# Threshold attention into Fourier mixing: the first stretch's bank-emptying additions move between the exponentials and the maskings

## The chip, the cores and the metric

The kernel runs on one core of a Trainium2 chip. The metric is device time in microseconds of one execution. The kernel before takes 1631.21 us, the median of 3 runs (1630.87 to 1632.28). The profiled execution took 1630.36 us, and its span from the first to the last instruction is 1628.5 us.

Engines are called by the profile's names: PE is TensorE (PEld its weight loads), DVE is VectorE, ACT is ScalarE, POOL is GpSimd, SP issues the transfers.

## What is computed

Two blocks follow one another, for 8 batches of 576 rows:

```python
scores = scale * q @ k.T                    # 8 heads of 64, 576 x 576
thresh = max(scores) - tau
scores = where(scores >= thresh, scores, -1e9)
attn = exp(scores - max(scores));  attn = attn / (sum(attn) + 1e-9)
x = attn @ v                                # heads put side by side: 576 x 512
mixed = real(fft(fft(x, axis=1), axis=2))   # "mixing"
u = x + mixed
un = (u - mean(u)) / sqrt(var(u) + 1e-6)
out = u + relu(un @ w_ch1) @ w_ch2          # 512 -> 2048 -> 512, "channels"
```

All of it is in fp32.

## The kernel before, in words

**Attention.** Two heads make a pair and four pairs a batch. A pair is worked off in five steps (`t` is 0 to 4), each for 128 query rows of both heads (the fifth holds the last 64 rows of both). Steps are numbered `i`, 20 to a batch, 160 in all. In a step of the main loop (from batch 2 on, `i` from 40) this is done:

- `scores(i)` (L427, L433): PE writes the scores of the two heads into two PSUM tiles `sc`. The tag has two buffers, so the next step's scores need the tiles of this step back.
- `softmax_first(i)`: DVE takes the row maxima `neg` (L506), ACT the exponentials `e` (L512) and, between the two of them, the threshold `thr` (L516).
- `softmax_second(i)`: DVE masks the exponentials by comparing `sc` with `thr`, and sums them into `den` (L527, "the maskings"); then it adds 1e-9 (L531) and takes the reciprocal (L534).
- `softmax_third(i)`: ACT multiplies the weights by the reciprocal (L540).
- `weights_in_parts(i - 1)`: PE transposes the weights of the step before (`pe` L578, `pw` L596), and ACT copies them out (L584, L598).
- `values_in_parts`, at `t` 1 and 3: PE multiplies by v (`pv`, L627), ACT copies the result to `x` (L634). For the first pair of a batch the target is called `x_first`.

**Channels.** The two products of the channel block are done in groups of 512 rows. All but the first group are done by a two-level fast scheme with seven products on each level (`two_level`). The first half of a group makes units `ph` (L1163, 8 matmuls, one bank): each bank is emptied by an ACT copy, or by a DVE addition into `hs` (`add`, L1100) that an ACT relu follows (L1105). The second half makes units `po` (L1304, 8 matmuls, seven units to a product): a bank is emptied after units 3 and 6, by an ACT copy (L1319) or a DVE addition (L1321, L1324). Beside them run jobs with no bank: sums of h for the next product (L1144, L1121, L1109, on DVE and POOL; kept in `side` for a unit's slot), the closing additions of a group (L1211 on POOL, L863 on DVE; kept in `pending`, two for each `tick()`, or in `side`), and after unit 3 of the first four products `rows.load`, which transposes 128 rows of u (`pn`, L836), copies them (L841, L842) and takes their statistics (L844, L845).

**Mixing.** When a batch's attention is done, `mixing(b)` makes its Fourier transform in units: three that fold the rows on DVE (L709, L710, L731 to L740), then matmuls `py` (L750) and `pa` (L767, L771), then sums into `u_t` (L787 to L796). The first is put out at the step with `i % 20 == 2`, by `start_batch`.

**The order of the work.** The schedule is written by hand: each engine runs its instructions in the order in which the Python code puts them out. What fills the PE between the attention's own matmuls is put out by `fill()`, three times in a step ("stretches"). Each call raises a `budget` by `per_slot`, takes one unit of the mixing if there is one (`mix(1)`), and then takes channel units from `work` until `spent`, counted in PE columns, has reached the budget. A `ph` unit counts 4096 columns, a `po` unit 2048, a py or pa unit `MIX / 11`. The main loop puts out, in a step:

```python
scores(i); next(values, None)               # PE: sc, and pv at t 1 and 3
softmax_first(i); softmax_second(i)
next(values, None)                          # ACT: x <- pv
fill()                                      # first stretch
next(weights, None)                         # pe and pw of the step before
fill()                                      # second stretch
next(weights, None); softmax_third(i)       # second pw, then the scaling
fill()                                      # third stretch
```

The small banks (tag `mm`: pe, pw, pv, ph, po, py, pa, pn) go round four buffers in the order in which they are asked for. The second `pw` is asked for before the second stretch, though its matmuls come after it.

Of the kernel before, what the change touches and what calls it, by code (L numbers as in the profile page):

```python
# [47 lines left out]
def kernel(  # L48
# [368 lines left out]
    def scores(i):  # L417
        n, t = divmod(i, NT)
        qT, kT = heads[n][0:2]

        nh = 2 if t < 4 else 1
        sc = [ps.tile([128, 2, 512], FP32, tag="sc", name=f"sc{j}") for j in range(nh)]
        if t < 4:
            for c in range(2):
                for j in range(2):
                    hp, k0 = slice(64 * j, 64 * j + 64), D * (1 - j)
                    nc.tensor.matmul(  # L427
                        sc[j][:, c, 0:HALF], qT[hp, 128 * t : 128 * t + 128],
                        kT[hp, k0 + HALF * c : k0 + HALF * (c + 1)], start=True, stop=True,
                    )  # L430
        else:
            for c in range(2):
                nc.tensor.matmul(  # L433
                    sc[0][:, c, 0:HALF], q_ends[:, :], kT[:, D + HALF * c : D + HALF * (c + 1)],
                    start=True, stop=True,
                )
        steps[i] = (sc, nh)
# [84 lines left out]
    def softmax_second(i):  # L522
        sc, nh, e, thr = steps[i]
        den = sb.tile([128, 2], FP32, tag="den", bufs=3, name="den")
        for j in range(nh):
            ej = e[:, S * j : S * (j + 1)].rearrange("p (c n) -> p c n", c=2)
            nc.vector.scalar_tensor_tensor(  # L527
                out=ej, in0=sc[j][:, :, 0:HALF], scalar=thr[:, j : j + 1], in1=ej,
                op0=ALU.is_ge, op1=ALU.mult, accum_out=den[:, j : j + 1],
            )  # L530
        nc.vector.tensor_scalar(  # L531
            out=den[:, 0:nh], in0=den[:, 0:nh], scalar1=1e-9, scalar2=None, op0=ALU.add
        )
        nc.vector.reciprocal(den[:, 0:nh], den[:, 0:nh])  # L534
        steps[i] = (nh, e, den)

    def softmax_third(i):
        nh, e, den = steps[i]
        for j in range(nh):
            nc.scalar.activation(  # L540
                out=e[:, S * j : S * (j + 1)], in_=e[:, S * j : S * (j + 1)], func=ACT.Copy,
                scale=den[:, j : j + 1],
            )
        if nh == 1:
            nc.scalar.copy(e[:, S : S + 64], e[:, 512:S])
        steps[i] = (e, None)
# [495 lines left out]
    def block(g, second, index):  # L1042

        n = len(LOADS) * (g - 1) + (7 if second else 0) + index // PER
        if index % PER == 0:
            ensure(n + 2 if g > 1 or second or index < 20 else n + 1)
        return w1[n % 3][:, 512 * (index % PER) : 512 * (index % PER + 1)]
# [14 lines left out]
    def two_level(g, rows):  # L1062
# [44 lines left out]
        def s1_part(part):  # L1107
            c = slice(512 * part, 512 * part + 512)
            nc.gpsimd.tensor_tensor(  # L1109
                out=s1_tile[:, c], in0=quadrant(0, 1)[:, c], in1=quadrant(1, 1)[:, c], op=ALU.add  # L1110
            )
# [88 lines left out]
                s1_part(part)  # L1200
        for _ in forms:
            pass
        while pending:
            tick()
        if g == 1:
            for part in range(4):
                s1_part(part)
# [41 lines left out]
        side = {}  # L1249
# [45 lines left out]
        for at, m in enumerate(L1):  # L1295
            for jn, j in enumerate(J):
                cut = g == NG - 1 and m == 3
                if jn in (0, 4) or cut and jn > 4:
                    bank = ps.tile([128, 512], FP32, tag="mm", bufs=4, name="po")
                c0 = 0 if cut and jn > 4 else 128 * (jn % 4)  # L1300
                to = bank[:, c0 : c0 + 128]
                right_ = block(g, True, 7 * at + jn)
                for s in range(4):
                    nc.tensor.matmul(  # L1304
                        to, lefts[m][j][:, s], right_[:, 128 * s : 128 * (s + 1)],
                        start=(jn in (0, 4) or cut and jn > 4) and s == 0, stop=s == 3,
                        skip_group_check=True,
                    )
                if jn in (3, 6) or cut and jn > 3:
                    first, end = (0, 512) if jn == 3 else (512, NV)  # L1310
                    if cut and jn > 3:
                        first, end = 128 * jn, 128 * jn + 128
                    src = bank[:, 0 : end - first]

                    def here(v):
                        return v[:, first:end]

                    if m in (1, 5, 4):
                        nc.scalar.copy(here({1: v_u, 5: v_22, 4: v_21}[m]), src)  # L1319
                    elif m == 2:  # L1320
                        V.tensor_tensor(out=here(v_11), in0=here(v_u), in1=src, op=ALU.add)  # L1321
                    else:
                        to = here(v_12 if m == 3 else v_u)
                        V.tensor_tensor(out=to, in0=to, in1=src, op=ALU.add)  # L1324
                for job in side.get((at, jn), ()):
                    job()
                if jn == 3 and at < 4:
                    rows.load((2, 3, 0, 1)[at])
                    if at == 3:
                        wanted.append(rows)  # L1330
                    yield ND * 128
                if jn < 6:
                    yield 2048
            background()
            if m != 3:
                yield 2048
# [14 lines left out]
    pending = []  # L1351
    wanted = []

    def tick():

        for _ in range(2):
            if pending:
                pending.pop(0)()

    def settle(b):  # L1360

# [8 lines left out]
    def background():  # L1370

        if late:
            fold_more()

    late = []
    ended = []


    mixes = []
# [2 lines left out]
    spent = budget = per_slot = 0.0  # L1382
    per_batch = NPAIR * NT

    def fill():
        nonlocal budget, spent
        budget += per_slot
        if mixes and not ended:
            mix(1)
        while work and spent < budget and work[0][0] < mixed:  # L1390
            done = next(work[0][1], None)
            if done is None:
                work.pop(0)
            else:
                spent += done
        if mixes and ended:
            mix(1)

    total = B * per_batch
# [117 lines left out]
    def fold_more():  # L1517
        if folds and next(folds[0], True):
            folds.pop(0)
# [16 lines left out]
    def mix(count):  # L1536
        nonlocal spent, mixed
        for _ in range(count):
            done = next(mixes[0], None)
            if done is None:  # L1540
                mixes.pop(0)
                mixed += 1
                break
            spent += done
# [76 lines left out]
    for i in range(2 * per_batch, total + 3):  # L1621


        n, t = divmod(i, NT)
        values = iter(())
        if i < total:
            scores(i)
        if t == 3 and i < total:
            values = values_in_parts(n, 0)
        elif t == 1 and n > 0:  # L1630
            while folds:
                fold_more()
            values = values_in_parts(n - 1, 1)
        next(values, None)
        if i < total:
            softmax_first(i)
            softmax_second(i)
        next(values, None)
        if i % per_batch == 2:
            for _ in last_fold:  # L1640
                pass
            start_batch(i // per_batch - 1)
        fill()
        if t == 1:
            if n % NPAIR:
                folds.append(fold_rows(n - 1))
            else:
                last_fold = fold_rows(n - 1)
                next(last_fold)
        weights = weights_in_parts(i - 1) if i <= total else iter(())  # L1650
        next(weights, None)
        if t > 2:
            fold_more()
        fill()
        if i % per_batch == 1:
            next(last_fold)
        next(weights, None)
        if i < total:
            softmax_third(i)
            if t == 1:  # L1660
                prep_ends(n)
            if t == 2 and n + 1 < B * NPAIR:
                scale_q(n + 1)
            if t == 3 and n + 1 < B * NPAIR:
                prep_pair(n + 1)
        if wanted:
            wanted.pop().factors()
        if i % per_batch == 1:
            next(last_fold)
        fill()  # L1670
        if t == 2 and n + 1 < B * NPAIR:
            load_v(n + 1)
        if t == 4 and n + 2 < B * NPAIR:
            load_pair(n + 2)
# [50 lines left out]
```

## Time and profile before

| | busy us | share of 1628.5 us |
|---|---|---|
| DVE | 1101.7 | 68% |
| ACT | 907.7 | 56% |
| POOL | 813.2 | 50% |
| DMA queue q1, share of 16 engines | | 48.5% |

PE stands in the prediction's first lines. By time the execution falls into three parts: up to 290 us the first two batches' attention, from 290 to 1385 us the main loop that the change touches, and after it the last groups of the channel block with no attention beside them.

| stretch, us | length | PE busy | DVE busy | mean granted PE clock |
|---|---|---|---|---|
| 0 to 290 | 290.0 | 260.39 | 237.51 | 0.97 |
| 290 to 1385 | 1095.0 | 1063.18 | 719.94 | 0.98 |
| 1385 to 1628.5 | 243.5 | 226.32 | 144.22 | 0.98 |

A row of the profile's groups reads: line, engine, operation, output<-input, shape, count, then busy time, the mean of one in ns, and the idle time of that engine just before such an instruction with the releaser that ended most of it. A row of the timeline reads: start, duration, engine, line, operation, and in brackets the idle time before it with what ended it.

### The profile page before, as it was taken

The numbers are of one execution on the slowest core, as the hardware profiler recorded it, in microseconds if no ns is written. First come the engines' busy times: TensorE is split into PE (matmuls) and PEld (weight loads), VectorE is DVE, ScalarE is ACT, GpSimd is POOL, SyncE is SP. The second block draws the span as 40 slices with busy tenths as digits, with TensorE's granted clock in tenths as the row PEclk, the third lists the DMA queues.
The fourth block names the chain that finished last, engine by engine and source line by source line (L and its number), as shares of the span: only waits on it lengthen the run. The fifth ranks groups of instructions, "written<-read, shape, count | busy, mean of one in ns | idle before, by whom it ended". The sixth has DMA issues, their size and how long they took to land.

```text
span 1628.5 us, 27053 instructions
## 1 busy us (share of the span) xinstructions
PE 1549.9 (95%) x9770; PEld 1194.2 (73%) x9770; DVE 1101.7 (68%) x2165; ACT 907.7 (56%) x1873; POOL 813.2 (50%) x1014
## 2 busy tenths in 40 slices
PE   8998989999999999989999999999998999999997
PEld 4555445556787777877787878877787778879997
DVE  7997786846769466765577566856576666646547
ACT  5774665554555666646665566556665665223131
POOL 6784664034355642545253724554264625546646
PEclk9999999999999999999999999999999999999999
DMA  6423221655846354634554354635464434536655
GB/s 160 125 56 113 74 75 36 196 158 161 266 156 189 102 157 125 187 91 139 139 166 143 112 131 147 178 100 152 126 186 120 136 119 146 209 135 234 239 201 188
DMA packets 245498, 239.04 MB, mean 147 GB/s; under 512 B 196947, under 2 KB 214869, under 8 KB 225014
## 3 DMA queue, kind: packets, MB, share of 16 engines
q1 hardware_dynamic: 242854, 237.02, 48.5%
q8 instruction: 78, 1.28, 0.3%
q10 hardware_dynamic: 2512, 0.30, 0.2%
q14 instruction: 54, 0.44, 0.1%
HBM read 207.50 MB, written 29.62 MB: 146 GB/s over the span
## 4 chain that ended last, share of the span: by engine, by line
PE 67%; DVE 18%; ACT 9%; issue 3%; POOL 2%; DMA 1%; SPq 0%; DVEq 0%; ACTq 0%; POOLq 0%
PE ph L1163 19%; PE po L1304 16%; PE pv L627 8%; PE sc L427 7%; PE pw L596 5%; PE po L901 3%; ACT e L512 2%; PE ph L877 2%; DVE e L527 2%; DVE e L467 2%; DVE hs L1100 2%; PE py L750 1%; DVE neg L506 1%; PE pa L767 1%; ACT hs L1105 1%
## 5 line engine op out<-in xcount | busy, mean ns | idle before, releaser
L506 DVE TENSOR_REDUCE neg<-sc 128x1 f32<-128x576 f32 x216 | 154.2, 751 | 133.9 <-PE sc L427 112.1
L512 ACT ACTIVATE e<-sc,neg 128x576 f32<-128x576 f32 x216 | 158.6, 734 | 152.5 <-DVE neg L506 152.0
L1304 PE MATMUL po<-w,w_all 128*128 128x128 f32 x1792 | 227.9, 277 | 1.0 <-DVE w_all L1144 0.7
L1304 PEld LDWEIGHTS po<-w,w_all 128*128 128x128 f32 x1792 | 213.0, 192 | 10.5 <-issue 8.5
L527 DVE SCALAR_TENSOR_TENSOR e<-sc,thr,e 128x576 f32<-128x576 f32 x216 | 169.1, 816 | 69.6 <-ACT thr L516 69.6
L1109 POOL TENSOR_TENSOR w<-hs 128x512 f32<-128x512 f32 x32 | 41.6, 1303 | 338.4 <-ACT hs L1105 319.2
L1100 DVE TENSOR_TENSOR hs<-ph,hs 128x512 f32<-128x512 f32 (+1 forms) x128 | 105.0, 821 | 140.0 <-PE ph L1163 90.8
L596 PE MATMUL pw<-ident,e 128*128 128x128 f32 x1152 | 175.5, 280 | 21.8 <-ACT x_first L634 11.3
L1163 PE MATMUL ph<-u_t,w 128*128 128x256 f32 x768 | 182.8, 385 | 3.5 <-ACT ends L584 2.0
L598 ACT COPY e_t<-pw 128x512 f32<-128x512 f32 x256 | 148.5, 593 | 65.6 <-PE pw L596 64.6
L427 PE MATMUL sc<-kT,qT 64*128 64x288 f32 x1024 | 169.8, 434 | 9.6 <-DVE e L467 8.3
L596 PEld LDWEIGHTS pw<-ident,e 128*128 128x128 f32 x1152 | 137.7, 144 | 44.0 <-ACT x_first L634 12.9
L1163 PEld LDWEIGHTS ph<-u_t,w 128*128 128x128 f32 x768 | 142.1, 191 | 29.4 <-issue 4.9
L1163 PE MATMUL ph<-w_all,w 128*128 128x256 f32 x672 | 157.0, 382 | 2.9 <-DVE hs L1100 1.8
L540 ACT ACTIVATE e<-e,den 128x576 f32<-128x576 f32 x216 | 157.8, 776 | 2.1 <-DVE den L534 1.7
L1105 ACT ACTIVATE hs<-hs 128x512 f32<-128x512 f32 (+1 forms) x96 | 74.1, 772 | 139.7 <-DVE hs L1100 139.1
L1163 PEld LDWEIGHTS ph<-w_all,w 128*128 128x128 f32 x672 | 123.5, 190 | 25.6 <-issue 5.3
L427 PEld LDWEIGHTS sc<-kT,qT 64*128 64x128 f32 x1024 | 93.3, 187 | 64.0 <-issue 32.1
L1211 POOL TENSOR_TENSOR w_all<-w_all 128x128 f32<-128x128 f32 (+2 forms) x160 | 119.4, 763 | 24.5 <-DVE w_all L1321 11.0
L1304 PE MATMUL po<-w,hs 128*128 128x128 f32 x960 | 130.5, 284 | 0.0
L1304 PEld LDWEIGHTS po<-w,hs 128*128 128x128 f32 x960 | 120.6, 199 | 5.1 <-issue 4.1
L792 POOL TENSOR_TENSOR u_t<-x,tmp 128x289 f32<-128x289 f32 (+1 forms) x45 | 34.9, 775 | 94.3 <-DVE tmp L787 94.3
(221 smaller groups left out, 2980.7 us busy)
## 6 DMA issues: line engine op xcount, KB each, us to landing
w<-f SPq DMA_DIRECT2D x152, 1024.0 KB, 4.9
hs<-in_moe_w_ch_dram SPq DMA_DIRECT2D x23, 512.0 KB, 4.7
q_in<-in_q_dram SPq DMA_DIRECT2D x128, 72.0 KB, 4.0
out_dram<-u SPq DMA_DIRECT2D x36, 256.0 KB, 2.6
k_in<-in_k_dram SPq DMA_DIRECT2D x124, 72.0 KB, 3.0
v_in<-in_v_dram SPq DMA_DIRECT2D x64, 128.0 KB, 4.6
f<-w SPq DMA_DIRECT2D x14, 512.0 KB, 3.4
f<-w SPq DMA_DIRECT2D x7, 1024.0 KB, 4.8
```

Source lines behind the costliest of these rows:

```text
L427: nc.tensor.matmul(sc[j][:, c, 0:HALF], qT[hp, 128 * t : 128 * t + 128], kT[hp, k0 + HALF * c : k0 + HALF * (c + 1)], start=True, stop=True,)
L506: nc.vector.tensor_reduce(out=neg[:, j : j + 1], in_=sc[j][:, :, 0:HALF], axis=AXIS_XY, op=ALU.max, negate=True,)
L512: nc.scalar.activation(out=ej, in_=sc[j][:, :, 0:HALF], func=ACT.Exp, bias=neg[:, j : j + 1], scale=1.0)
L527: nc.vector.scalar_tensor_tensor(out=ej, in0=sc[j][:, :, 0:HALF], scalar=thr[:, j : j + 1], in1=ej, op0=ALU.is_ge, op1=ALU.mult, accum_out ...
L540: nc.scalar.activation(out=e[:, S * j : S * (j + 1)], in_=e[:, S * j : S * (j + 1)], func=ACT.Copy, scale=den[:, j : j + 1],)
L596: nc.tensor.transpose(pw[:, c, :], e[:, c0 : c0 + 128], ident[:, :])
L598: nc.scalar.copy(e_t[:, 4 * j : 4 * j + 4, qs], pw[:, :, :])
L627: nc.tensor.matmul(pv[64 * j : 64 * j + 64, 0:m], vt[:, 2 * c + j, :], e_t[:, 4 * j + c, 0:m] if c < 4 else ends[:, 0, 0:m], start=(c == 0 ...
L1100: nc.vector.tensor_tensor(out=to, in0=bank, in1=to if other is None else other, op=ALU.add)
L1163: nc.tensor.matmul(bank[:, 256 * q : 256 * q + 256].rearrange("p (two n) -> p two n", two=2), left[:, 256 * c + 128 * q : 256 * c + 128 * ...
L1211: return lambda: eng.tensor_tensor(out=to, in0=to, in1=other, op=ALU.add)
L1304: nc.tensor.matmul(to, lefts[m][j][:, s], right_[:, 128 * s : 128 * (s + 1)], start=(jn in (0, 4) or cut and jn > 4) and s == 0, stop=s == ...
```

## The change

In the main loop the first stretch is put out between the exponentials and the maskings. `fill(True)` sets a flag `holding`. While it is set, jobs of `side` and of `pending` are not run when their turn comes but gathered in a list `held`; what is held is put out behind the next unit, and what is left behind the maskings. The mixing's unit is not taken inside such a fill but behind the maskings and the held jobs. So on DVE the additions that empty a bank (and the statistics of `rows.load`, and work that a unit puts out itself) stand between `neg` and the maskings, and the sums of h, the closing additions and the mixing's work behind them. It is for emptying the banks sooner and for giving DVE work while it waits for the exponentials. Outside a held fill the new lists empty at once and the order is as before; the second and third stretch, the first two batches and the end are put out as before. No operation is added or removed.

```diff
-        while pending:
+        while pending or held:
             tick()
+            while held:
+                held.pop(0)()
...
-                for job in side.get((at, jn), ()):
-                    job()
+                while held:
+                    held.pop(0)()
+                held.extend(side.get((at, jn), ()))
+                while held and not holding:
+                    held.pop(0)()
...
     def tick():
 
+        while held:
+            held.pop(0)()
         for _ in range(2):
             if pending:
-                pending.pop(0)()
+                held.append(pending.pop(0))
+        while held and not holding:
+            held.pop(0)()
...
-    def fill():
+    holding = []
+    held = []
+
+    def fill(hold=False):
         nonlocal budget, spent
+        holding[:] = [True] if hold else []
         budget += per_slot
-        if mixes and not ended:
+        if mixes and not ended and not hold:
             mix(1)
         while work and spent < budget and work[0][0] < mixed:
...
+        holding.clear()
         if mixes and ended:
             mix(1)
...
         if i < total:
             softmax_first(i)
-            softmax_second(i)
         next(values, None)
         if i % per_batch == 2:
             for _ in last_fold:
                 pass
             start_batch(i // per_batch - 1)
-        fill()
+        fill(True)
+        if i < total:
+            softmax_second(i)
+        while held:
+            held.pop(0)()
+        if mixes:
+            mix(1)
```

## The prediction

> **What bounds the kernel now.** I read the page first, then what PE waits for in the main loop, then the windows and the chain of waits around its longest waits. The page gives PE:
>
> ```profile
> PE 1549.9 (95%) x9770; PEld 1194.2 (73%) x9770; DVE 1101.7 (68%) x2165; ACT 907.7 (56%) x1873; POOL 813.2 (50%) x1014
> ```
>
> PE is the bound, so only what PE stands still, or runs slowly, can be won. In the main loop (290 to 1385 us) it is idle 1095.0 - 1063.2 = 31.8 us. The waits of PE in that stretch (who waited for whom; total, times, longest):
>
> ```profile
> PE pw L596 <- ACT x_first L634: 11.3, 6, 2.3
> PE py L750 <- DVE f L731: 8.5, 10, 2.0
> PE ph L1163 <- DVE hs L1100: 3.4, 4, 2.0
> PE pw L596 <- DVE hs L1100: 2.4, 2, 2.1
> PE ph L1163 <- ACT ends L584: 2.0, 11, 0.4
> ```
>
> There are two kinds. Rows one and two (19.8 us) lie where a batch's mixing begins (five places, 525 to 1237 us). Rows three to five (7.8 us) are waits for a bank of the first half of a group, scattered. Each longer wait costs again through the clock; windows of 3.41 us (PE busy is the second number, the granted clock the third from the end):
>
> ```profile
> 1052.34:1055.75 3.41, 2.49 (x20) 1.46 (x16) 3.41 (x4) 0.00 (x0) 2.30 (x2) 1.00 0.08 18
> 1055.75:1059.16 3.41, 1.68 (x11) 1.33 (x11) 3.30 (x7) 0.68 (x2) 1.30 (x1) 1.00 0.21 31
> 1059.16:1062.58 3.42, 2.23 (x11) 2.23 (x12) 3.04 (x8) 2.59 (x9) 0.77 (x1) 0.50 0.68 275
> 1062.58:1065.99 3.41, 3.41 (x18) 2.72 (x17) 1.85 (x4) 1.48 (x3) 0.00 (x0) 0.50 0.24 59
> ```
>
> A window in which PE is busy about half leads to a window at half clock; 6.8 us at half clock cost 3.4 us. Four of the five batches (700, 881, 1059, 1236 us) have two such windows, the one at 526 us has one.
>
> The chain of waits there, start and duration:
>
> ```profile
> 1047.30 1.58 DVE e L527 x4
> ...
> 1057.71 0.68 DVE neg L506
> ...
> 1059.30 0.73 ACT e L512
> 1060.03 0.27 ACT x_first L634
> ...
> 1060.35 1.11 PE pw L596 x4
> ```
>
> It is a chain on DVE: without a gap from the maskings at 1047.30 through the mixing's first folds and sums to the next step's `neg`, then exponentials, then `x_first`, which frees the bank that `pw` needs. The scores had been ready since 1051.7 us.
>
> A wait of the second kind, on DVE and then on PE in the timeline:
>
> ```profile
> 427.47 0.75 DVE L506 TENSOR_REDUCE neg<-sc 128x1 f32<-128x576 f32 x1
> 429.21 0.82 DVE L527 SCALAR_TENSOR_TENSOR e<-sc,thr,e 128x576 f32<-128x576 f32 x1 [0.99 <-ACT thr L516]
> 430.34 0.67 DVE L1100 TENSOR_TENSOR hs<-ph,hs 128x512 f32<-128x512 f32 x1
> 431.07 0.68 PE L596 MATMUL pw<-ident,e 128*128 128x128 f32 x2 [2.11 <-DVE hs L1100]
> ```
>
> PE had finished that bank at about 426.7 us; the addition stood behind a masking that waited 0.99 us for its threshold.
>
> [...] L735 takes 1.55 us and L731 1.53 us at 1052 to 1055 us, while POOL runs L1144 and L1121; their shortest are 0.47 and 0.52 us.
>
> **The change, part by part.** It moves work, so PE's busy time at full clock stays.
>
> *Additions ahead of the maskings.* DVE waits for `thr` 69.6 us in 120 steps; that time can hold the addition, but DVE is not the bound, so only PE's waits count. At 407.80 (1.01), 431.07 (2.11), 757.63 (0.27) and 765.81 us (1.95), 5.3 us together, the addition was ready before the maskings and stood behind them. Two maskings with their sums take 1.6 us, `den` 0.4 us, the wait for `thr` 0.4 to 1 us: 2.4 to 3 us, more than each wait. I take 4.8 of the 5.3 us. The eleven waits on ACT `ends` (2.0 us, plus 0.3 at a po unit): the copy stands on ACT behind a relu that waits for such an addition; I take 1.8. The window at half clock from 431.12 us goes with the wait of 2.11 us: 1.7. Sum: 8.3 us.
>
> *Order of mixing and channel unit on PE.* At the step where PE first multiplies for the mixing (`py`, 1053.96 us), the order is now pv, py (waits 0.64 and 1.01 us for DVE), one po unit of 1.06 us, pe, then 2.19 us of idle time until `pw`. The budget of a stretch is (19,240 + 217,088) / 60 = 3939 columns. py counts 1749, so one po unit follows (1749 + 2048 = 3797; three stretches of two units before it overran by 3 x 157, so 3468 suffice). With the mixing behind, two units (4096) go first, and the next stretch gets none. PE thus does one unit of 1.06 us more before the wait ends. If `neg` comes when it comes now, that is 1.06 us for each of five batches.
>
> *When this `neg` comes.* Plus 0.7 us: two steps earlier, the first stretch holds a `rows.load`. Its statistics wait for ACT's copies (until 1038.9 us), and the maskings, now 1035.60 to 1037.16, then come behind them, at about 1039.9 to 1041.5; `den` is ready at 1041.9, so ACT's scaling starts at 1041.9 instead of 1041.31, and behind it the table loads and `rstd` on which DVE waits anyway. Minus 0.4 us: in the step of 1045.50 us a sum of h (L1144, 0.68 us) falls into the wait of 0.39 us for `thr`. Minus 0.5 us: that sum is ready sooner, so POOL's L1144 and L1121 start while DVE masks, which reads PSUM (0.82 us with POOL busy and without)[...]. Bounds: +0.7 and -1.8; I take -0.2. So 5 x 1.26 = 6.3 us.
>
> *Clock at these places.* The idle time falls from 3.84 to about 2.6 us, mostly in one piece. Whether it leads to no, one or two slow windows depends on where their edges fall. I take one fewer in 60% of four batches: 4 x 1.7 x 0.6 = 4.1 us (bounds 0 and 15).
>
> *Maskings later.* They now wait for a PE unit. Behind the masking wait `den`, ACT's scaling, and the next scores for the `sc` tiles. Worst common step: scores at 1101.3, pv, unit from 1104.80 to 1106.7. The maskings, now at 1104.50, would start at 1106.7 + 0.1 + 0.67 = 1107.5 and end at 1109.1; the next scores are at 1111.08 us. Hidden, with 2 us to spare. Without pv the delay is 0.7 to 1.3 us with 2.3 us to spare (1123.92 to 1126.19). With a wide addition (1.22 us), a `rows.load`, or weight forms (L945, L977, which a unit puts out unheld) the margin shrinks to almost nothing. I charge 3 us.
>
> *At no cost:* held closing additions (L863, L1211) and sums of h: needed eight units later or by a store. After 1385 us the order is the old one.
>
> Sum: 8.3 + 6.3 + 4.1 - 3 = 15.7 us; 1631.2 - 15.7 = 1615.5 us.
>
> **Rivals.**
>
> 1. *The mixing's start doesn't move.* DVE's chain gets longer through the statistics, eats the one unit, and the clock drops twice as before. For it: DVE is without a gap there. Against it: the wait for `thr` is in the same chain. Left: 8.3 - 2 = 6 us, so 1625 us.
> 2. *The clock no longer drops.* [...] the idle time falls under half a window: 8.3 + 5 x 2 + 15 - 1 = 32 us, so 1599 us. Against it: `neg` to `pw` alone takes 2.6 us, in which PE has little but pe.
> 3. *The maskings become the bound (slower).* If half of the 120 steps let the scores wait 0.4 us, 24 us are lost against 8.3 us won: 1647 us. For it: margins near 2 us and PE at 97% in the loop. Against it: PE shows no wait for L527 now, and the worst step above still closes.
> 4. *Gain and new waits cancel:* 1631 us.
>
> **How the numbers follow.** Forecast 0.56, rival one 0.22, two 0.08, three 0.08, four 0.06. Faster by over 0.2% (under 1627.9 us): 0.86; within 0.2%: 0.06; slower: 0.08. The range goes from 1602 us (forecast with all of the clock) to 1630 us (only part of the bank waits): it leaves out rivals two and three and part of four.
>
> **What would show it.** Right: the waits of PE for L1100 in the loop fall from 5.8 us to under 1 us and no slow window is left at 431 us; two po units between pv and py at each mixing's start, and fewer slow windows there. Wrong: PE waits for `sc` on L527 (rival three); that step's `neg` still 12.1 us behind the `neg` before it (1045.58 to 1057.71) and two slow windows in each batch (rival one); new waits behind `rows.load` or weight forms beyond 3 us.

## The result and the profile after

The changed kernel takes 1605.7 us (median of 3 runs, 1603.82 to 1607.52) against 1631.21 us (1630.87 to 1632.28): a ratio of 0.9842, 95% interval 0.982 to 0.9864. That is 25.5 us less, where 15.7 us were forecast: the direction was right, the time lies inside the range and near its fast end. A later study with the same kernel gave 1605.14 us and 0.984 (0.9826 to 0.9855).

The profile page's line of busy times, after:

```profile
PE 1537.4 (96%) x9770; PEld 1189.2 (74%) x9770; DVE 1105.6 (69%) x2165; ACT 908.4 (57%) x1873; POOL 811.7 (51%) x1014
```

PE has the same 9770 instructions and 12.5 us less of busy time. No work went, so these 12.5 us were time in which PE's records were longer: at half clock, or behind a wait (shown below). From the first masking of the loop to its last, the kernel before took 1083.6 us (PE idle 31.8), the changed one 1058.6 us (idle 19.8). So 25.0 us were won in the loop; outside it the two traces differ by 0.3 us the other way.

Who PE waited for after, from 290 to 1385 us (total, times, longest):

```profile
PE pw L596 <- ACT x_first L634: 9.1, 5, 2.2
PE pe L578 <- DVE w_all L1326: 5.2, 5, 2.6
...
PE pw L596 <- ACT ends L584: 1.5, 3, 0.5
...
PE ph L1163 <- DVE hs L1100: 0.3, 1, 0.3
```

Line numbers from 1200 to 1326 have moved by two: L1326 is the addition that was L1324. The waits for L1100 fell from 5.8 us to 0.3 us. The waits at the mixing's start are still the longest: the row of `x_first` is only smaller (11.3 before), and a wait of `pe` stands where `py` waited for L731. (A last wait of `py` for L731, 2.9 us at 1384 us, lies behind the loop. The kernel before has it too, 2.6 us at 1410 us, and so outside the stretch of its list.)

The wait that the prediction showed at 431 us, on DVE and PE in the timeline after:

```profile
425.80 0.75 DVE L506 TENSOR_REDUCE neg<-sc 128x1 f32<-128x576 f32 x1
426.47 0.68 DVE L1100 TENSOR_TENSOR hs<-ph,hs 128x512 f32<-128x512 f32 x1
427.50 0.60 PE L596 MATMUL pw<-ident,e 128*128 128x128 f32 x4
428.27 0.81 DVE L527 SCALAR_TENSOR_TENSOR e<-sc,thr,e 128x576 f32<-128x576 f32 x1
```

The addition L1100 now runs directly behind `neg`, while DVE would have waited for the exponentials, and `pw` starts without a wait.

The chain of waits at the mixing's start at 1040 us, after:

```profile
1030.30 1.49 DVE e L527 x4
1031.78 0.02 issue
1031.81 1.18 DVE den L531
...
1038.77 0.68 DVE neg L506
...
1041.09 0.27 ACT x_first L634
1041.36 0.04 issue
1041.40 0.67 PE pw L596 x4
```

It is the same chain as before: DVE without a gap from the maskings to `neg`, then the exponentials, then `x_first`. What changed is how much PE has to do ahead of it: two `po` units (from 1035.64) and `py`, and then it stops twice, close together, for 0.56 us before `pe` and 2.19 us before `pw`: 2.75 us, where it had stopped three times for 3.84 us. This `neg` starts 11.52 us behind the one before it (1027.17 to 1038.69), where it had been 12.13 us (1045.50 to 1057.63).

The windows of 3.41 us there (PE busy is the second number, the granted clock the third from the end):

```profile
1035.08:1038.50 3.42, 3.28 (x28) 2.67 (x24) 3.39 (x9) 0.24 (x1) 0.00 (x0) 1.00 0.25 38
1038.50:1041.91 3.41, 0.81 (x5) 0.56 (x5) 3.41 (x5) 2.38 (x7) 2.07 (x1) 1.00 0.85 346
1041.91:1045.33 3.42, 3.42 (x17) 2.69 (x16) 3.31 (x10) 2.57 (x6) 0.00 (x0) 0.50 0.02 5
1045.33:1048.74 3.41, 3.41 (x27) 3.20 (x27) 1.66 (x3) 1.74 (x4) 1.27 (x1) 1.00 0.44 71
```

One window in which PE was busy for 0.81 us was followed by one window at half clock, where two followed before. In the loop there are four such windows (at 520, 694, 1042 and 1216 us) instead of ten.

### The profile page after: what moved, and what is told of

It reads as the page before. It is cut to its first block, busy times and chain, and to the rows that moved or that the text cites. A ratio compares the mean times of both kernels' runs of the same rounds, so it can differ in the third digit from the quotient of the medians.

```text
span 1603.8 us, 27061 instructions
## 1 busy us (share of the span) xinstructions
PE 1537.4 (96%) x9770; PEld 1189.2 (74%) x9770; DVE 1105.6 (69%) x2165; ACT 908.4 (57%) x1873; POOL 811.7 (51%) x1014
## 4 chain that ended last, share of the span: by engine, by line
PE 76%; DVE 14%; ACT 4%; issue 2%; POOL 2%; DMA 1%; SPq 0%; DVEq 0%; ACTq 0%; POOLq 0%
PE ph L1163 24%; PE po L1306 17%; PE pv L627 8%; PE sc L427 7%; PE pw L596 6%; PE po L901 4%; PE ph L877 2%; PE py L750 2%; DVE e L467 2%; PE sc L433 1%; PE pa L767 1%; PE pe L578 1%; PE pa L771 1%; DVE neg L451 1%; ACT e L512 1%
## 5 line engine op out<-in xcount | busy, mean ns | idle before, releaser
L1100 DVE TENSOR_TENSOR hs<-ph,hs 128x512 f32<-128x512 f32 (+1 forms) x128 | 105.1, 821 | 158.5 <-PE ph L1163 104.0
L596 PE MATMUL pw<-ident,e 128*128 128x128 f32 x1152 | 172.1, 276 | 18.0 <-ACT x_first L634 9.1
L527 DVE SCALAR_TENSOR_TENSOR e<-sc,thr,e 128x576 f32<-128x576 f32 x216 | 168.1, 811 | 17.7 <-ACT thr L516 17.7
L540 ACT ACTIVATE e<-e,den 128x576 f32<-128x576 f32 x216 | 157.6, 775 | 16.6 <-DVE den L534 15.4
L1306 PE MATMUL po<-w,hs 128*128 128x128 f32 x960 | 126.3, 279 | 0.0
L1306 PEld LDWEIGHTS po<-w,hs 128*128 128x128 f32 x960 | 116.2, 193 | 9.4 <-issue 7.2
```

The source lines that it names most:

```text
L527: nc.vector.scalar_tensor_tensor(out=ej, in0=sc[j][:, :, 0:HALF], scalar=thr[:, j : j + 1], in1=ej, op0=ALU.is_ge, op1=ALU.mult, accum_out ...
L540: nc.scalar.activation(out=e[:, S * j : S * (j + 1)], in_=e[:, S * j : S * (j + 1)], func=ACT.Copy, scale=den[:, j : j + 1],)
L596: nc.tensor.transpose(pw[:, c, :], e[:, c0 : c0 + 128], ident[:, :])
L1100: nc.vector.tensor_tensor(out=to, in0=bank, in1=to if other is None else other, op=ALU.add)
L1306: nc.tensor.matmul(to, lefts[m][j][:, s], right_[:, 128 * s : 128 * (s + 1)], start=(jn in (0, 4) or cut and jn > 4) and s == 0, stop=s == ...
```

## The experiments

Two theories had to be told apart. **A**: the prediction's sum, about half from banks emptied sooner and half from the mixing's start. **B**: nearly all from one of the two. The expectations name two rivals more, **C** (about 0.2 us in every step alike) and **D** (at the mixing's start it is the maskings' new place on DVE that wins, not the order on PE). Then the terms inside were tested: PE's order, the statistics, the margin of the maskings, and what holds the rest of the idle time at the mixing's start. Where a gain is given by step, it is how far the start of that step's scores on PE moved, against the kernel compared with.

### The new order only where no mixing runs

```diff
+        old = bool(mixes) or i % per_batch == 2
...
+            if old:
+                softmax_second(i)
...
-        fill(True)
+        if old:
+            fill()
+        else:
+            fill(True)
```

(In the `else` follow the maskings, held jobs and mixing's unit as in the change.)

> New order in the steps with no mixing under way, old order in the others. Theory A (the gain has two parts, bank waits outside the mixing and one po unit more ahead of the mixing's gap): the waits for a bank outside the mixing and the slow window at 431 us go, 8 to 10 us won, so 1621 to 1624 us, with seven or more slow windows left in the loop. Rival B (all of the gain comes from the order around the mixing): 1630 to 1632 us. Rival C (the gain comes from the maskings' place in all steps alike, about 0.2 us a step): some 70 of 120 steps, 1615 to 1618 us.

Measured: 1612.77 us (1610.79 to 1614.0) against 1630.33 us, ratio 0.9889 (0.9873 to 0.9905): 17.6 us. That is twice what theory A gave this part, and too much for B's version in which it gives nothing. Rival C's 1615 to 1618 us comes nearer, but most steps don't move at all. The gain lies at the steps where the whole change gains outside the mixing, and has nearly the same amounts, 17.2 us in all: 1.73 and 3.67 us where the two waits near 408 and 431 us were, 1.65 us at 766 us, and 0.78 us at each of nine steps (70, 75, 95, 110, 115, 130 and so on) where PE's row of waits had shown 0.2 us. Besides, three of the mixing's starts gained 0.75 to 1.22 us and four steps lost 0.44 us each (a new wait, see the statistics below): 1.1 us together. Why these starts gain, with the old order in them, was not tested.

So where do 0.78 us come from, when PE was seen to wait 0.16? From the weight loads, whose rows the prediction had not read. The waits of PEld in the kernel before, 290 to 1385 us:

```profile
PEld pw L596 <- DVE hs L1100: 8.3, 12, 2.5
...
PEld ph L1163 <- DVE hs L1100: 4.9, 5, 2.2
PEld ph L1163 <- ACT ends L584: 4.0, 10, 0.4
```

Where PEld has the first row with 8.3 us in twelve waits, PE's own row had 2.4 us in two. One such place in the timeline before:

```profile
1113.77 0.27 PE L578 MATMUL pe<-ident,e 128*128 128x128 f32 x1
...
1116.35 0.42 PEld L596 LDWEIGHTS pw<-ident,e 128*128 128x128 f32 x4 [0.54 <-DVE hs L1100]
1116.35 0.66 PE L596 MATMUL pw<-ident,e 128*128 128x128 f32 x4
...
1117.16 1.59 PEld L1163 LDWEIGHTS ph<-u_t,w 128*128 128x128 f32 x8 [0.40 <-ACT ends L584]
1117.17 1.99 PE L1163 MATMUL ph<-u_t,w 128*128 128x256 f32 x8 [0.16 <-ACT ends L584]
...
1119.09 0.51 PE L427 MATMUL sc<-kT,qT 64*128 64x288 f32 x2
```

and the same step after:

```profile
1092.94 0.27 PE L578 MATMUL pe<-ident,e 128*128 128x128 f32 x1
...
1095.00 0.57 PEld L596 LDWEIGHTS pw<-ident,e 128*128 128x128 f32 x4
1095.21 0.60 PE L596 MATMUL pw<-ident,e 128*128 128x128 f32 x4
...
1095.65 1.89 PE L1163 MATMUL ph<-u_t,w 128*128 128x256 f32 x8
...
1097.47 0.51 PE L427 MATMUL sc<-kT,qT 64*128 64x288 f32 x2
```

From `pe` to `pw` it takes 2.58 us before and 2.27 after; from `pw` to the scores 2.74 and 2.26. The sum is 0.79 us, and only 0.16 of it is an idle time of PE. The reason lies in how the records follow each other. The ends of matmuls are modelled, and after, without a wait, `pw`'s record (1095.21 + 0.60 = 1095.81) runs 0.16 us past the start of the unit behind it (1095.65). A wait must first eat up this overlap before the row of PE shows any of it: before, `pw` ends at 1117.01 and `ph` starts at 1117.17, which is shown as 0.16 us and is 0.32 us lost. The wait of `pw` itself, 0.31 us lost, isn't on PE's row at all, while its load waited 0.54 us. Behind a wait the records are also longer (0.66 for 0.60, 1.99 for 1.89 us). 0.31, 0.32, 0.06 and 0.10 make the 0.79 us.

### The new order only where a mixing runs

```diff
+        old = not mixes and i % per_batch != 2
```

(the rest as in the kernel above)

> New order only in the steps with mixing under way. Theory A: the rest of the gain, 15 to 18 us, so 1613 to 1616 us; the wait at 431 us and the one of 1.95 us are still there. Rival B: 1605 to 1608 us. Rival C: 1618 to 1621 us.

Measured: 1621.86 us (1619.7 to 1622.57), ratio 0.9943 (0.9928 to 0.9959): 8.5 us, at the steps behind a mixing's start (0.58, 2.33, 1.12, 2.22 and 2.59 us). That is half of what theory A gave this part: A had the two parts, but not their sizes. Rival C's 1618 to 1621 us is near once more, but all of the gain lies at five steps. With 17.6 us this makes 26.1 us against 25.5 us for the whole. The two parts add, as nearly as the clock's windows let one tell.

### PE's order alone

Of the kernel before, only the mixing's unit behind the first stretch's channel units; maskings and additions where they were.

```diff
-    def fill():
+    def fill(mix_last=False):
...
-        if mixes and not ended:
+        if mixes and not ended and not mix_last:
...
-        if mixes and ended:
+        if mixes and (ended or mix_last):
...
-        fill()
+        fill(True)
```

> The maskings stay ahead of the first stretch, as in the kernel before; only the mixing's unit is taken behind the channel units of the first stretch. Theory A: the one po unit more ahead of the gap is won here too, 5.3 us for five batches plus 2 to 8 us of slow windows, so 1618 to 1624 us. Rival D (at the mixing's start it is the shorter chain on VectorE, made by the maskings' place, that wins): within 2 us of the kernel before, 1629 to 1632 us.

Measured: 1625.57 us (1623.69 to 1629.72, 6 runs), ratio 0.9975 (0.9958 to 0.9991): 4.8 us on medians, between theory A's range and D's. The trace is of the fastest of these runs. In it the five steps behind the mixing's start gain 2.58, 0.60, 1.82, 2.41 and 1.32 us, 8.7 us in all, as much as with the new order where a mixing runs (8.8 us in its trace). Part of both is the clock, which differs from run to run (0.981 to 0.988 in these six). PE's idle time alone, in two steps at each start, falls from 20.0 us to 16.5 us here and to 15.7 us there. So at the mixing's start the order on PE gives most of the gain; whether the 0.8 us that are left come from the maskings' new place was not tested. Elsewhere this kernel has the old waits; its trace lost 1.7 us to a window at half clock at 762 us that the kernel before just missed (there PE was busy for 1.66 us of the window from 762.20 us, and the next one was at 1.00), and won 1.4 us because the one at 431 us is absent.

### x_first's copy ahead of the exponentials

```diff
+        early = i % per_batch == 3
+        if early:
+            next(values, None)
         if i < total:
             softmax_first(i)
-        next(values, None)
+        if not early:
+            next(values, None)
```

> The changed kernel, and in the step with i % 20 == 3 the copy of pv to x_first stands ahead of the exponentials on ScalarE. Theory A (the gap that is left, 2.2 us before pw in each of five batches and the slow window behind it, hangs on this copy, which frees the bank): 11 us of idle time and up to four slow windows (6.8 us) go: 1588 to 1595 us, no slow window at a mixing's start. Rival E (with the copy out of the way PE waits just as long for the next thing that VectorE owes, the bank that L1326 empties or the next scores): 1603 to 1607 us.

Measured: 1605.5 us (1602.47 to 1607.09), ratio 0.9843 (0.9826 to 0.986): no gain, as rival E had it. The wait for `x_first` is gone, and its place is taken by the next copy that stands behind the exponentials on ACT. PE's waits, 290 to 1385 us:

```profile
PE py L750 <- ACT y_e L760: 8.5, 6, 2.0
```

So freeing the chain's last link wins nothing by itself: the next copy stands behind the same exponentials, and these wait for `neg`.

### The statistics behind the maskings

```diff
-            nc.vector.bn_stats(stats[:, :], u[:, :])
-            nc.vector.bn_aggr(self.mv[:, t, :], stats[:, :])
+            def statistics():
+                nc.vector.bn_stats(stats[:, :], u[:, :])
+                nc.vector.bn_aggr(self.mv[:, t, :], stats[:, :])
+
+            held.append(statistics)
+            while held and not holding:
+                held.pop(0)()
```

(and `held` is emptied before `rows.factors()`)

> The changed kernel with one thing undone: the statistics of rows.load (L844, L845) are held behind the maskings like the sums of h, so the maskings no longer stand behind a wait for ACT's copies. Theory (the maskings' delay by the statistics is paid in part at the mixing's start, +0.7 us in five batches, and in part by a new wait of pw for ACT's ends, 0.44 us in four steps): 1600 to 1604 us. Rival (DVE waits for rstd later in that step anyway, so the statistics' place costs nothing): as the changed kernel, 1604.5 to 1607.

Measured: 1604.77 us (1604.37 to 1605.36), ratio 0.9837 (0.9823 to 0.9852), beside 1605.14 us for the changed kernel on the same chip. Both theories were half right. The waits of `pw` for ACT's `ends` are gone and the four steps gain their 0.44 us each. But the mixing's start hardly moves: `pw` still waits 9.0 us for `x_first`, and of the 0.7 us that the prediction charged there 0.2 us was paid (`neg` comes 25.75 us behind the scores of two steps before, and 25.95 us in the changed kernel). The 1.8 us won don't show in the time: this trace has six windows at half clock at the mixing's starts and not four, though PE waits no longer there (mean granted clock of the trace 0.985, of the changed kernel's two 0.988 and 0.987). What brought the two more was not shown. The further 0.95 us at one step is no effect of the statistics; the next kernel has it too.

### The changed kernel again

The changed kernel without an edit, as the measure for the others.

> The changed kernel once more, beside the other three, for their comparison: 1604 to 1607 us, ratio 0.984 to 0.986. If slow windows are set by where the windows' edges happen to fall, its trace may show another number of them in the loop than the four of the first trace, with a span that differs by about 1.7 us for each.

Measured: 1605.14 us (1604.28 to 1606.63). Its trace has the same four windows at half clock in the loop. That doesn't show that they are no matter of chance: the kernel with the statistics held has six, though PE waits no longer in it. One wait of the first trace (`pw` for `x`, 0.8 us near 416 us) is absent: that step starts 0.95 us sooner.

### The maskings one stretch later

```diff
         fill(True)
-        if i < total:
-            softmax_second(i)
...
         fill()
+        if i < total:
+            softmax_second(i)
```

> The changed kernel with the maskings moved on by one more stretch: behind pe, pw and the second stretch. Theory (a masking that waits for a first-stretch unit is hidden only because it ends about 2 us before the next scores need the sc tile): the second stretch is some 2 to 4 us of PE work, so in most steps PE waits for sc on L527, 0.4 us or more in 120 steps, 1640 to 1690 us, with PE's waits naming L527 or the scaling behind it. Rival (there is far more slack than the 2 us, since the bank waits are all that the order changes): within 4 us of the changed kernel.

Measured: 1673.23 us (1672.51 to 1674.33), ratio 1.0257 (1.0239 to 1.0274): 68 us slower than the changed kernel. The mechanism of the slower rival is real, and the change stops one stretch short of it. It is not the whole of the 68 us: five steps at the mixing's starts lose 6.3 to 7.6 us each, 36 us in all, and there PE waits mostly for ACT's copies `ends` and L1321, and the clock drops more often (13 windows at half clock in the loop; its mean granted clock is 0.98, the changed kernel's 0.99). PE's waits and those of its weight loads, 290 to 1425 us, first PE:

```profile
PE sc L427 <- DVE e L527: 21.2, 22, 3.7
```

then PEld:

```profile
PEld sc L427 <- DVE e L527: 48.0, 75, 3.9
```

PE's row shows 22 waits; the loads show 75, and 47 steps lose 0.5 to 1.4 us each, 37 us in all. Whoever read PE's row alone would again have seen too little.

### The whole stretch ahead of neg

At the step behind the mixing's start, `x_first`'s copy, the first stretch, the held jobs and the mixing's unit stand ahead of `softmax_first`.

```diff
+        early = i % per_batch == 3
+        if early:
+            next(values, None)
+            fill(True)
+            while held:
+                held.pop(0)()
+            if mixes:
+                mix(1)
         if i < total:
             softmax_first(i)
...
```

(further down these parts are left out at that step)

> The changed kernel; only at the step behind the mixing's start (i % 20 == 3) x_first's copy, the first stretch, the held jobs and the mixing's unit stand ahead of neg and the exponentials, so no copy of y_e, e or x stands behind an exponential there. Theory (the remaining 2.2 us before pw, with 0.56 us before pe, is the exponentials' place on ACT ahead of the copies that PE needs, at five places, with one slow window each): 1585 to 1594 us, four or five waits of pw for x_first gone. Rival (as with the copy alone, the idle time only moves to the next wait, for w_all on DVE or the exponentials now later): 1602 to 1608 us.

Measured: 1621.27 us (1619.69 to 1621.44), ratio 0.9936 (0.9921 to 0.9951): 16 us slower than the changed kernel, a miss for both theories. The timeline at that step:

```profile
1049.52 2.45 DVE L1144 TENSOR_TENSOR w_all<-w_all,hs 128x512 f32<-128x512 f32 x1
...
1051.90 1.41 DVE L506 TENSOR_REDUCE neg<-sc 128x1 f32<-128x576 f32 x2
...
1054.50 0.47 PE L596 MATMUL pw<-ident,e 128*128 128x128 f32 x1 [4.28 <-ACT ends L584]
```

The held sums of h now stand ahead of `neg`: it starts 9.6 us after its scores began (1042.28), against 6.5 us in the changed kernel, and the copy of `ends` stands behind the exponentials in place of `x_first`'s, so `pw` waits 4.28 us and not 2.19. This points to a cause: what delays `neg` on DVE is paid by PE.

### Folds behind neg

From this a theory **F**: what remains at the mixing's start is DVE's backlog ahead of `neg`. Its test puts DVE's third fold unit (L731 twice, L740) behind `neg`, and the first `py` behind `pe` and `pw`; `x_first` is copied first as above.

```diff
         fill(True)
+        if starts:
+            mix(1)
         if i < total:
             softmax_second(i)
...
         next(weights, None)
+        if starts:
+            mix(1)
...
-        fill()
+        fill(folds_wait=i % per_batch == 2 and i < total)
```

(`starts` is `i % per_batch == 3 and i < total`; with `folds_wait` a stretch takes no mixing unit.)

> The changed kernel, other only at the mixing's start in six batches: the third fold unit on DVE (L731 twice, L740; 1.4 us) is put out behind the next step's neg instead of ahead of it, x_first's copy ahead of the exponentials, and the first py unit behind pe and the first pw. Theory F (what remains at the mixing's start is DVE's backlog ahead of neg: den, four folds and additions): neg comes 1.4 us sooner, pw no longer waits for x_first, and py waits 1 to 1.5 us for the folds instead of 2.75 us before pe and pw: 1.2 us in five batches and one slow window fewer in some, 1596 to 1600 us. Rival E (as with the copy alone, the idle time only changes its name): 1603 to 1607 us, the same total of waits in the loop.

Measured: 1602.68 us (1601.44 to 1605.9), ratio 0.9836 (0.982 to 0.9853). The timeline there:

```profile
1037.43 1.42 DVE L506 TENSOR_REDUCE neg<-sc 128x1 f32<-128x576 f32 x2
...
1038.76 1.51 DVE L1144 TENSOR_TENSOR w_all<-hs 128x512 f32<-128x512 f32 x1
1040.19 0.97 DVE L731 SCALAR_TENSOR_TENSOR f<-f,factors 128x304 f32<-128x304 f32 x2
1040.77 0.49 PE L750 MATMUL py<-dim_c,f 128*128 128x128 f32 x2 [2.13 <-DVE f L731]
```

`neg` comes 1.26 us sooner (1037.43, not 1038.69) and `pw` waits for nothing, as F says. But the idle time is now `py`'s, and in the loop it is 18.7 us, where the second trace of the changed kernel has 19.0 us; so far this is rival E. Between `neg` and the folds stands a sum of h of 1.51 us, which the first stretch puts out behind its second unit. The ratio is 0.9836 against 0.984, and the intervals overlap: not told apart from no change.

The next kernel puts the first `py` behind the second stretch's channel units as well, with one mixing unit more in the third stretch. Against the kernel above:

```diff
-        if starts:
-            mix(1)
...
-        fill()
+        fill(folds_wait=starts)
+        if starts:
+            mix(1)
...
+        if starts:
+            mix(1)
```

> As the kernel with the folds later, and the first py unit also behind the second stretch's channel units, with one unit of the mixing more in the third stretch. Theory F (DVE's backlog; with two more units of 1.06 us ahead of py the folds are ready in time): waits at the mixing's start under 1 us for each batch, hardly a slow window there, 1586 to 1594 us. Rival E: the idle time moves on, to the second pw, to sc behind later maskings or to the next py unit, 1600 us or more.

Measured: 1609.38 us (1608.84 to 1610.18), ratio 0.9871 (0.9856 to 0.9886): rival E, slower than the changed kernel by 4 us. PE's waits:

```profile
PE py L750 <- DVE w_all L1326: 9.2, 4, 2.3
PE py L750 <- DVE f L731: 5.5, 4, 1.4
```

The bank of the later `py` is one whose addition L1326 comes behind the maskings on DVE.

> As the kernel with py later, and with the statistics of rows.load held behind the maskings. Theory: the two do not touch, and the waits of pw for ACT's ends (0.44 us in four steps, 0.95 us in one) go again: 2.7 us less than the kernel with py later, more or less 1.7 us for each slow window by which they differ. Rival (DVE at the mixing's start gets the held statistics in its way): as the kernel with py later or slower.

That kernel with the statistics held too: 1608.78 us (1605.57 to 1611.44), ratio 0.9866 (0.9852 to 0.9881). The waits for `ends` go, the difference of 0.6 us is within the runs' spread: inconclusive on the time.

### Folds directly behind neg

The folds kernel again (the first of the last three), with the fold unit ahead of the first stretch and so ahead of the sum of h, and with the statistics held.

```diff
-        fill(True)
         if starts:
             mix(1)
+        fill(True)
...
```

> As the kernel with the folds later, with the third fold unit directly behind neg, ahead of the first stretch (a sum of h, L1144, of 1.5 us stood between them), and with the statistics of rows.load held behind the maskings. Theory F: py's waits of 2.1 and 0.4 us for the folds fall to 0.7 to 1.2 us together in four or five batches (1.3 us each), and the statistics give 0.44 us at the same four steps and 0.95 us at one as before: 1593 to 1597 us, with three or four slow windows in the loop. Rival E (the idle time moves on): the loop's waits stay above 16 us and the time between 1600 and 1605 us.

Measured: 1594.52 us (1593.57 to 1595.88, 5 runs) against 1631.07 us, ratio 0.9778 (0.9765 to 0.9792). That beats both kernels: its interval lies below that of the changed kernel (0.9826 to 0.9855 in the closest study) by some 10 us. PE's waits from 290 to 1385 us:

```profile
PE py L750 <- DVE f L731: 8.9, 5, 2.9
PE py L750 <- ACT ends L584: 2.0, 1, 2.0
PE py L750 <- DVE f L740: 1.7, 4, 0.4
```

The timeline at the same place as above:

```profile
1032.37 1.41 DVE L506 TENSOR_REDUCE neg<-sc 128x1 f32<-128x576 f32 x2
...
1033.70 1.75 DVE L731 SCALAR_TENSOR_TENSOR f<-f,factors 128x304 f32<-128x304 f32 x2
...
1035.06 0.49 PE L750 MATMUL py<-dim_c,f 128*128 128x128 f32 x2 [1.50 <-DVE f L731]
```

In the loop PE is idle 12.3 us (19.0 in the second trace of the changed kernel, 18.7 with the folds behind the sum of h), and at the five mixing's starts only two windows are at half clock (863 and 1208 us) instead of four (mean granted clock of the loop 1.00, in the changed kernel 0.99). Three of the five starts have none. The three steps with a window at half clock fewer gain 2.47, 3.68 and 2.25 us over the first trace of the changed kernel; the other two 1.03 and -0.72; the four steps with the `ends` 0.44 each. F holds: DVE's order around `neg` was what PE waited for. Of the idle time won, 1.8 us belong to the statistics. How much of the windows at half clock that went, some 3.7 us, is owed to the order was not shown.

## Why the prediction was right, and where its sum was off

The gains below are by step from the two traces of before and after; they sum to 24.9 us, and the spans of the two traces differ by 24.7 us. New waits are listed apart.

| term | forecast us | measured us |
|---|---|---|
| banks emptied sooner, with the window at 431 us | 8.3 | about 17.0 |
| mixing's start: order, `neg`, clock | 6.3 + 4.1 | about 10.8 |
| new waits | -3 | about -2.9 |

**Banks: the mechanism was right, the size forecast was half of what came.** The step that failed is the term "I take 1.8" for the eleven waits on `ends`, and with it "only PE's waits count". They were read from PE's rows (2.0 us). In truth nine of these steps gained 0.78 us each, and three near 745 to 770 us 0.46, 0.51 and 1.65: 9.7 us where 1.8 and about 2 had been taken. In the batch of the weight forms the two long waits and the window at half clock gave 1.73 and 3.65 us, near the 4.5 us taken (0.9 of 3.12, and 1.7); three more steps there gave 0.50, 0.52 and 0.98 us with no row of PE to announce them. The rows of PEld would have told: the loads' waits for L1100 shown above, with those for `ends`, fall from 17.2 us to 1.0 us in the same rows:

```profile
PEld ph L1163 <- DVE hs L1100: 0.5, 1, 0.5
PEld ph L1163 <- ACT ends L584: 0.5, 2, 0.4
```

With 1.7 us for the window at half clock that makes 17.9 us. The kernel with the new order only outside the mixing gained 17.2 us at these steps.

**Mixing's start: the mechanism was right, and the sum too, with luck in its parts.** Two units now stand ahead of `py`, as worked out from the budget, and PE's order alone gave most of it. The idle time at the start near 1040 us fell by 1.09 us, where 1.26 us were taken. The shift of `neg` that was taken at -0.2 us measures so: from the scores of two steps before to `neg`, 26.13 us before (1031.50 to 1057.63) and 25.95 after (1012.74 to 1038.69). Its parts were less right. The statistics cost 0.2 us there and not 0.7. L735 and L731 do run at 0.48 and 0.53 us now, with POOL idle beside them (1032.95 to 1038.91 us); but `den`, which takes 0.17 us otherwise, takes 1.17 us at 1031.81 us, while POOL runs L1121 from 1031.68 to 1032.95. The prediction's 0.5 us for this place was an estimate from the 2.1 us by which the two exceed their shortest at 1052 to 1055 us before. In the end the clock gave a bit more than forecast (nine windows at half clock at the starts became four; PE was busy for 53 to 73% of four of the nine and for nearly all of the others, which at half of the busy time makes 12.8 us, and the four after cost 6.6: 6.2 us against 4.1), the idle time a bit less (rows of 20.5 us became 15.4 us, so 5.1 against 6.3). That the clock's term came near its forecast is luck: kernels in which PE waits alike at the starts have four such windows or six (the changed one and the one with the statistics held).

**New waits: right in size, partly for other reasons.** 0.44 us at four steps (`pw` behind `ends`, by the statistics) and 1.09 us once make 2.85 us; in the second trace the last is nearly gone, which leaves 1.9, and its cause stays open. No wait of PE for L527 in the loop (0.5 us in two waits of the loads) shows that the worst step did close, and the kernel with the maskings one stretch later shows what it costs where it doesn't.

**Rivals.** One falls: the starts moved. The time lies nearer to two's 1599 us than to the forecast, but not by two's cause: its 15 us of clock at the mixing's start were about 6, and the surplus came from the banks. That this surplus brings the time near to rival two's is chance. Three falls for this change, but its mechanism was produced at will. Four falls.

## What to carry to other kernels

Read the waits of the weight loads (PEld) beside those of PE: where matmuls' ends are modelled, a short wait hides in a stretched record, and here nine places shown with 0.2 us each were worth 0.78 us each. If an engine's wait only changes its name when its last link is moved, as with `x_first`, go back along the chain to the engine that has no gap, and reorder there: work that nobody waits for soon goes behind the one instruction that feeds the chain. It must not go too far back, either: with the folds behind `neg` and a sum of h nothing was won, with the folds directly behind `neg` (and the statistics held) another 10 us.

## What the runs showed of the hardware

In the traces of before and after, every window of the loop at full clock in which PE was busy for 44% or less was followed by one at half clock (before 36, 38 and 44%; after 23, 23, 24 and 36%), and none with 55% or more was (the lowest: after 55% at 867.79 us, before 62%). Between these before had four: two of 49% and one of 53% were followed by one at half clock, the fourth of 49%, at 762.20 us, was not. So the prediction's "about half" held at three places and failed at one. In either trace all windows at half clock begin on one grid of 3.413 us to within 3 ns; counted from the trace's start it lies at 1.03 us before and at 0.85 us after. After, at the start near 866 us (same columns as above):

```profile
864.38:867.79 3.41, 2.20 (x19) 1.85 (x17) 3.41 (x8) 0.33 (x1) 0.95 (x1) 1.00 0.55 180
867.79:871.21 3.42, 1.88 (x16) 1.60 (x17) 3.35 (x8) 3.26 (x10) 1.12 (x1) 1.00 0.50 204
871.21:874.62 3.41, 3.41 (x28) 3.01 (x27) 3.18 (x6) 2.38 (x7) 1.27 (x1) 1.00 0.00 0
```

PE idles 2.7 us here too, spread over two windows, and the clock stays whole. Near 1040 us, in the windows shown further up, 2.6 us fell into one window, and the next was at half clock. About the same idle time thus went once without a window at half clock and once with one. A gain of 1 or 2 us can thus be lost in the time to one or two more of them (half of 3.41 us each, if PE is busy throughout), as with the held statistics.

How long `den` took beside POOL differed with its width. In the trace after, POOL beside it at 1031.81 us:

```profile
1031.68 1.27 POOL L1121 TENSOR_TENSOR hs<-hs,w 128x512 f32<-128x512 f32 x1
1031.81 1.17 DVE L531 TENSOR_SCALAR den<-den 128x2 f32<-128x2 f32 x1
```

Of the 96 `den` with two columns, 30 took 0.36 to 1.42 us and ended within 0.03 us of an instruction of POOL that ran beside them; only four that began beside POOL took 0.17 us, and for them POOL's instruction ended within 0.15 us. Of the 24 with one column 20 began beside POOL, and none took over 0.16 us. Why the width matters the runs do not show.
